# Twelve head pairs in one loop, with batch 0's first product in one piece

## The chip, the cores and the metric

The kernel runs on one core of a Trainium2 chip. The metric is the device time of one execution in microseconds (us).

Engine names in the profile: PE is TensorE (PEld its weight loads), DVE is VectorE, ACT is ScalarE, POOL is GpSimd, SP is SyncE, which here issues the DMAs of q, k, v, of the output and of the transposes. POOL issues the DMAs of the weights.

## The reference

Attention over 8 batches, 12 heads, 448 positions and a head size of 64, with one added to each softmax denominator; its output, laid out as 3584 rows of 768, goes through a two-layer network with the Mish function (2048 wide).

```python
scores = scale * np.matmul(q, k.transpose(0, 1, 3, 2))
m = np.max(scores, axis=-1, keepdims=True)
e = np.exp(scores - m)
attn = e / (np.sum(e, axis=-1, keepdims=True) + np.exp(-m) + 1e-09)
attn_out = np.matmul(attn, v)

x = attn_out.transpose(0, 2, 1, 3).reshape(B * S, H * D)
h = x @ w_in
sp = np.where(h > 20.0, h, np.log1p(np.exp(np.minimum(h, 20.0))))
g = h * np.tanh(sp)
return g @ w_out
```

## The kernel before

**Pairs and steps.** Work goes by head pairs: 48 of them, six to a batch. A pair has seven 128-row tiles of scores (its two heads have 896 rows) and is done in four steps: three with two tiles, the last with one. A step's scores lie in one of three PSUM tiles of two banks (`sc_tiles`), taken in turn, so scores can be three steps ahead of the exps (`scores_ahead`).

**The life of a pair.** `load_pair` loads q, k, v in f32 (three DMAs on SP's queue). `cast_pair` makes bf16 of them (three GpSimd instructions). `transpose_pair` turns q and k on PE, and `evac_qk` brings them from PSUM to SBUF, scaled; from pair 12 on (`DIAG_FROM`) q is laid out blockwise with zeros, so that one matmul makes a tile for both heads, and VectorE writes it (two memsets for each of the first three such pairs, two scalings). `scores` issues PE's matmuls and VectorE's reduction for the row maximum (L270). `exps` issues ScalarE's exponentials (L283) with the row sums; after the last step comes `expm`, the exponential of the negated maximum. `denominators` adds and inverts on VectorE. `normalise` multiplies the seven tiles of `en` by the reciprocals (L317 on VectorE, or L315 on GpSimd after a small copy of the reciprocals, L308). Then `en` is turned into `eT`, by one DMA transpose on SP's queue (L321) or by PE (`turn_on_pe`: seven transposes for each of four blocks j, each copied out of PSUM by VectorE, L336). `av_pair` multiplies `eT` with v (eight matmuls, L358); its result is copied to `xT` (L367).

**The two products.** `mm1_mish` makes one 128-wide block of the first product out of `xT` (six matmuls, L382) and applies Mish on ScalarE (L388); a batch has 16 blocks. Mish and the exponential need different activation tables, so ScalarE loads a table at each change between them. `mm2_part` gives pieces of the second product (L446), to be put between other work.

**PSUM.** Besides the three score tiles there are two one-bank tiles `mo`, which q/k transposes, turns, `av` and the products share. A result that is to be copied out is put on the list `late`; `flush_late` issues these copies, and `mo_take` does so when no `mo` is free.

**The order.** No scheduler decides: each engine carries out its instructions in the order in which the program issues them (`manual_schedule`).

- Pairs 0 to 5 (`HEAD = HP`) go through a loop of their own. In step 0 of pair p, pair p+4 is loaded, p+3 is cast and one piece of a weight is loaded; pair p-1 is normalised in step 1; `av` of pair p-3 is issued in step 3.
- Then come units of three pairs. A unit runs the twelve steps of its pairs with pieces of the second product as filler between them (`plan`), and then eight blocks of the first product, behind which the three pairs are normalised and the q and k of the next unit are turned. Unit 2 (pairs 6 to 8) and unit 3 (pairs 9 to 11) have no filler and do the two halves of batch 0's first product. From unit 4 (`first_mm2`) on the second product runs along, and in units from there GpSimd normalises the third pair.
- PE turns pairs 5, 6 and 7 (`BY_PE`) during units 2 and 3; all others are turned by DMA.
- In these early units the `xT` copies are VectorE's; in the head loop they are ScalarE's (`act=True`).

The weight `w_in` comes in twelve pieces (a quarter of the columns, two of the six row blocks each), `w_out` in eight.

Of the kernel before, what the change touches and what calls it, by code (L numbers as in the profile page):

```python
# [9 lines left out]
FP32 = mybir.dt.float32  # L10
# [5 lines left out]
UNIT_PAIRS = 3  # L16
# [3 lines left out]
def kernel(  # L20
# [73 lines left out]
    DIAG_FROM = 2 * HP  # L94
    q_diag = [
# [32 lines left out]
    def w_pieces():  # L128
        c_in, c_out = d_ff // 4, NH
        for i in range(4):  # L130
            for a in range(0, DM_T, 2):
                yield (
                    w_in_sb[:, a : a + 2, i * c_in : (i + 1) * c_in],
                    moe_w_in[a * 128 : (a + 2) * 128, i * c_in : (i + 1) * c_in],
                )
# [31 lines left out]
    def transpose_pair(p, bank=None):  # L167
# [3 lines left out]
        ps = mo_take() if bank is None else sc_tiles[2][:, bank, :]  # L171
        ps_k = sc_tiles[1][:, bank, :] if bank is not None else mo_take() if p == 0 else ps
# [56 lines left out]
    def scores(idx):  # L229

        p, s = divmod(idx, STEPS)
        if s == 0:
            if p < HP or p % UNIT_PAIRS == 0:
                for nm in ("negm", "sums", "expm", "den", "rden"):
                    stats[nm] = st_pool.tile([128, UNIT_PAIRS, NTILE], FP32, tag=nm, name=nm)
            at = 0 if p < HP else p % UNIT_PAIRS
# [6 lines left out]
        if s == STEPS - 1 and p in av_with:  # L243
            av_pair(av_with.pop(p), bank=sc[:, 1, :])
# [30 lines left out]
    def exps(idx):  # L275
# [13 lines left out]
        if s == STEPS - 1 and p < HP:  # L289
# [12 lines left out]
    def normalise(p, dma=True, on_pool=False):  # L302
# [6 lines left out]
        for i in range(NTILE):  # L309
# [6 lines left out]
            else:  # L316
                nc.vector.tensor_scalar(scalar2=None, op0=ALU.mult, **args)  # L317
        eT = eT_pool.tile([128, NT, 2 * S], BF16, tag="eT", name="eT")
        st["eT"] = eT
        if dma:  # L320
            nc.sync.dma_start_transpose(  # L321
                out=eT.rearrange("c j (i q) -> c (j i) q", q=128),
                in_=en.rearrange("q j i c -> q (j i c)"),
            )

# [49 lines left out]
    def mm1_mish(b, ff):  # L375
# [3 lines left out]
        spare = ff % FF_U == 2  # L379
# [113 lines left out]
    W_AT = ({5: 1, 9: 1}, {1: 1, 5: 1, 7: 1, 9: 1, 11: 1}, {1: 1, 3: 1, 5: 1, 7: 1})  # L493
# [9 lines left out]
    cast_pair(2)  # L503


    for p in range(HEAD):
        for s in range(STEPS):
            if s == 1 and p == 0:
                transpose_pair(p + 2)
            exps(p * STEPS + s)  # L510
            if p == 0 and s == 0:
                evac_qk(1, act=True)
            if s == 1:
                evac_qk(p + 2, act=True)
            if s:
                flush_late()
            scores_ahead(HEAD * STEPS + 3)
            if s == (2 if p == HEAD - 1 else 0):
                load_pair(p + 4)
            if s == 0:  # L520
                cast_pair(p + 3)
                load_w(1)
                if p:
                    denominators(att[p - 1])
            if s == 1:
                if p:
                    normalise(p - 1)
            if s == 3 and p + 3 < HEAD + 2:
                transpose_pair(p + 3)
            if s == 3 and p >= 3:  # L530
                av_pair(p - 3, act=True)
    denominators(att[HEAD - 1])
    normalise(HEAD - 1, dma=HEAD - 1 not in BY_PE)

    for u in range(UNITS_PER_B, N_UNITS + 2 * UNITS_PER_B):
# [10 lines left out]
        for n in range(steps):  # L546
            pi, s = divmod(n, STEPS)
            p, idx = p0 + pi, p0 * STEPS + n
            late_tp = u == UNITS_PER_B and n == STEPS
            if late_tp:  # L550
                transpose_pair(p0 + 2)
            exps(idx)
            if late_tp:
                evac_qk(p0 + 2)
# [87 lines left out]
```

## Time and profile before

| | |
|---|---|
| median of 3 runs | 493.48 us (492.4 to 493.5) |
| the profiled execution | 492.95 us, its span 491.2 us, mean granted clock 0.99 |
| busy, share of the span | PE 92%, DVE 72%, ACT 71%, POOL 31% |
| DMA | 92.19 MB; hardware queue 81.7%, software queue 9.1% of 16 engines' time |
| exps of pairs 0 to 5 | 8.05 to 45.2 us |
| unit 2: exps, then product | 45.2 to 65.1, to 77.5 us |
| unit 3: exps, then product | 77.5 to 98.5, to 110.5 us |
| unit 4: exps | 110.5 to 125.6 us |

All details of the profile come from one execution, so times within it are set against its own 492.95 us. In a row of instruction groups, "x7" is the number of instructions and the figure before the engine's name their time together. The digits of a slice are tenths of its time.

### The profile page before, as it was taken

What the parts mean: (1) busy time and instruction counts of PE and PEld (TensorE: products, weight loads), DVE (VectorE), ACT (ScalarE), POOL (GpSimd) and SP (SyncE); (2) the same over time, 40 slices, a digit from 0 to 9 for tenths busy, and PEclk for the clock granted to TensorE, in tenths of its full rate; (3) what the DMA queues carried; (4) which work ended last, traced back from release to release, by engine and by line L of the source; (5) the groups of instructions that cost most, each with busy time, mean ns of one, the idle gap of its engine ahead of it and who ended that gap; (6) DMA issues with size and microseconds to landing.
All of it is one profiled execution on the core that took longest, in us unless ns stands there. A gap on an engine that the chain in (4) does not pass through costs nothing.

```text
span 491.2 us, 8805 instructions
## 1 busy us (share of the span) xinstructions
PE 451.8 (92%) x2992; PEld 249.3 (51%) x2992; DVE 352.7 (72%) x714; ACT 349.5 (71%) x906; POOL 152.1 (31%) x252
## 2 busy tenths in 40 slices
PE   4466995898999999999999999999999999999996
PEld 2222442454555555555555555556555565556563
DVE  4898987788868787878788786878797878420021
ACT  5988675768788887979697978888797979502300
POOL 4622270701433534252523324253435230300000
PEclk9999998799999999999999999999999999999999
DMA  8999999999999999899999979898999796780112
GB/s 221 207 211 214 245 212 154 239 166 223 190 231 249 215 226 195 240 187 250 147 247 198 216 175 206 209 216 234 176 260 174 170 177 141 132 157 21 45 37 93
DMA packets 209452, 92.19 MB, mean 188 GB/s; under 512 B 166272, under 2 KB 205952, under 8 KB 209408
## 3 DMA queue, kind: packets, MB, share of 16 engines
q1 hardware_dynamic: 201920, 85.35, 81.7%
q0 software_dynamic: 7488, 6.29, 9.1%
q8 instruction: 23, 0.38, 0.3%
q14 instruction: 21, 0.17, 0.1%
HBM read 45.61 MB, written 11.01 MB: 115 GB/s over the span
## 4 chain that ended last, share of the span: by engine, by line
PE 74%; DVE 10%; ACT 7%; DMA 6%; issue 2%; SPq 1%; POOL 0%; DVEq 0%; ACTq 0%
PE mo L446 26%; PE mo L382 24%; PE sc L249 9%; ACT en L283 6%; PE sc L358 6%; DVE negm L270 5%; DMA eT<-en 5%; PE sc L382 3%; DVE en L317 3%; PE sc L179 3%; PE mo L358 1%; DMA k_f<-in_k_dram 1%; DVE xT L367 1%; SPq L121 1%; PE mo L332 0%
## 5 line engine op out<-in xcount | busy, mean ns | idle before, releaser
L283 ACT ACTIVATE en<-sc,negm 128x448 bf16<-128x448 f32 x336 | 209.6, 638 | 31.9 <-DVE negm L270 14.5
L270 DVE TENSOR_REDUCE negm<-sc 128x2 f32<-128x896 f32 x192 | 182.6, 969 | 56.3 <-PE sc L249 44.9
L446 PE MATMUL mo<-w_out_sb,gT 128*128 128x384 bf16 (+1 forms) x896 | 142.1, 303 | 0.0
L382 PE MATMUL mo<-xT,w_in_sb 128*128 128x448 bf16 x672 | 140.3, 352 | 0.4 <-DVE xT L367 0.4
L388 ACT ACTIVATE gT<-mo 128x448 bf16<-128x448 f32 x112 | 59.4, 543 | 72.4 <-PE mo L382 72.2
L446 PEld LDWEIGHTS <-gT 128*128 128x128 bf16 x896 | 84.0, 98 | 46.8 <-issue 1.3
L382 PEld LDWEIGHTS <-w_in_sb 128*128 128x128 bf16 x768 | 72.8, 98 | 64.6 <-issue 3.8
L315 POOL TENSOR_SCALAR en<-en,rden 128x448 bf16<-128x448 bf16 x84 | 52.8, 650 | 93.8 <-DVE rden L308 86.9
L162 POOL CAST q_bf<-q_f 112x512 bf16<-112x512 f32 x47 | 28.9, 616 | 160.2 <-DMA q_f<-in_q_dram 151.1
L249 PE MATMUL sc<-kT,qd 128*128 128x448 bf16 x252 | 71.6, 354 | 1.5 <-DVE qd L210 0.7
L317 DVE TENSOR_SCALAR en<-en,rden 128x448 bf16<-128x448 bf16 x252 | 69.7, 347 | 0.9
L283 ACT ACTIVATION_READ_ACCUMULATOR en<-sc,negm 128x1 f32 x336 | 69.4, 207 | 0.0
L433 DVE COPY o_sb<-mo 128x384 f32<-128x384 f32 (+1 forms) x64 | 32.1, 502 | 41.3 <-PE mo L446 41.2
L249 PEld LDWEIGHTS <-qd 128*128 128x128 bf16 x252 | 23.9, 97 | 31.8 <-issue 13.8
L358 PE MATMUL sc<-eT,v_bf 112*64 112x448 bf16 x288 | 34.1, 357 | 2.0 <-ACT en L283 1.8
L164 POOL CAST v_bf<-v_f 112x512 bf16<-112x512 f32 x48 | 29.6, 616 | 15.4 <-DMA v_f<-in_v_dram 14.1
L255 PE MATMUL sc<-kT,qd 64*128 64x448 bf16 x36 | 17.7, 508 | 17.9 <-ACT en L283 16.1
L358 PEld LDWEIGHTS <-v_bf 112*64 112x64 bf16 x384 | 21.0, 115 | 25.4 <-issue 18.7
L163 POOL CAST k_bf<-k_f 112x512 bf16<-112x512 f32 x47 | 29.0, 617 | 5.1 <-DMA k_f<-in_k_dram 4.0
L210 DVE TENSOR_SCALAR qd<-sc 64x448 bf16<-64x448 bf16 x72 | 27.8, 386 | 0.9
L218 ACT COPY kT<-sc 128x448 bf16<-128x448 bf16 x39 | 20.8, 534 | 7.0 <-PE sc L179 7.0
L446 PE MATMUL mo<-w_out_sb,mid 128*128 128x384 bf16 x128 | 24.9, 326 | 0.0
(50 smaller groups left out, 307.3 us busy)
## 6 DMA issues: line engine op xcount, KB each, us to landing
q_f<-in_q_dram SPq DMA_DIRECT2D x48, 224.0 KB, 5.1
k_f<-in_k_dram SPq DMA_DIRECT2D x48, 224.0 KB, 5.3
v_f<-in_v_dram SPq DMA_DIRECT2D x48, 224.0 KB, 5.5
w_in_sb<-in_moe_w_in_dram POOLq DMA_DIRECT2D x12, 256.0 KB, 5.8
w_out_sb<-in_moe_w_out_dram POOLq DMA_DIRECT2D x8, 384.0 KB, 7.5
out_dram<-o_sb SPq DMA_DIRECT2D x7, 336.0 KB, 3.4
out_dram<-o_sb SPq DMA_DIRECT2D x8, 288.0 KB, 4.5
out_dram<-o_sb SPq DMA_DIRECT2D x8, 240.0 KB, 3.4
```

The source lines that it names most:

```text
L163: cast_k(out=k_bf, in_=k_f.rearrange(by_t, t=NT))
L164: nc.gpsimd.tensor_copy(out=v_bf, in_=v_f)
L249: nc.tensor.matmul(sc[:, bk, 0:S], lhsT=qT[:, i].rearrange("d h r -> d (h r)"), rhs=kT, start=True, stop=True,)
L270: nc.vector.tensor_reduce(out=negm, in_=sc[:, 0 : len(cols), 0:S], axis=AX.X, op=ALU.max, negate=True)
L283: nc.scalar.activation(out=st["en"][:, :, c, 0:SP_], in_=sc[:, bk, 0:S].rearrange("q (j c) -> q j c", j=NT), func=AF.Exp, bias=st["negm"][ ...
L315: nc.gpsimd.tensor_scalar(scalar2=1.0, op0=ALU.mult, op1=ALU.mult, **args)
L317: nc.vector.tensor_scalar(scalar2=None, op0=ALU.mult, **args)
L358: nc.tensor.matmul(av[h * 64 : (h + 1) * 64, 0:S], lhsT=v_bf[:, h, j * D : (j + 1) * D], rhs=e_h, start=(j == 0), stop=(j == NT - 1),)
L382: nc.tensor.matmul(h_ps[:, 0:S], lhsT=w_in_sb[:, dm, ff * 128 : (ff + 1) * 128], rhs=xT[b][:, dm, :], start=(dm == 0), stop=(dm == DM_T - 1),)
L388: nc.scalar.activation(out=gT[b][:, ff, :], in_=h_ps[:, 0:S], func=AF.Mish)
L433: nc.vector.tensor_copy(out=o_sb[:, cols], in_=st["o"][:, 0:n_cols])
L446: nc.tensor.matmul(st["o"][:, 0:n_cols], lhsT=src[:, ff, c0 : c0 + 128], rhs=w_out_sb[:, ff, cols], start=(ff == 0), stop=(ff == FF_T - 1),)
```

## The change

- `HEAD` becomes 12: the pairs of batches 0 and 1 all go through a new `head_pair`. Units begin at unit 4.
- Behind pair 6 (`FIRST` is 7) stands `first_product`: all 16 blocks of batch 0's first product. Blocks 0 and 1 start with five of six row blocks in a score tile's banks while pair 5's `av` is still to come. Pair 6 is normalised by VectorE there, pairs 7 and 8 have q and k turned there, and the first three scores of pair 7 are issued between the last blocks.
- In `head_pair`, GpSimd normalises the last three of seven tiles (`ON_POOL`), VectorE the first four: two in step 0, two in step 1. This concerns pairs 0 to 5 and 7 to 10; pairs 6 and 11 are normalised by VectorE alone.
- PE turns pairs 4, 5, 7 and 8, two blocks in step 2 and two in step 3 of the next pair; the other head pairs are turned by DMA.
- `av` of a pair that was turned by DMA is issued in step 2 of the third pair after it, of pair 4 in step 0 of pair 6; `av` of pairs 6 to 8 goes with the last scores of pairs 9 to 11, into a free bank. All but pair 5's `xT` copies among these are ScalarE's, and so are q's and k's evacuations of pairs 2 to 11.
- q and k of pairs 12 to 14 are turned in the steps of pairs 10 and 11 and of unit 4 instead of behind the first product.
- No pairs are loaded in the steps of pairs 3 to 6; `first_product` issues the loads of pairs 7 to 10 at once.
- Pieces of `w_in` are half of the columns by one row block; loads of both weights are spread anew (`W_AT`).
- The first piece of the second product (rows 0 to 127, half the columns, 16 matmuls) goes between the steps of pairs 10 and 11. Units 4 and 5 have two whole halves and three whole halves left, instead of two and a half and three and a half, and the two quarter pieces of 192 columns become one half piece.

The core of the diff; not shown are the new `w_pieces`, `HEAD` in place of `HP` in `scores` and `exps`, the choice of banks in `transpose_pair`, and `turn`, which is the second half of `normalise`:

```diff
+    def normalise_tiles(p, tiles, on_pool=False):
+        st = att[p]
+        en = st["en"]
+        if on_pool:
+            st["rden2"] = st_pool.tile([128, NTILE], FP32, tag="rden2", name="rden2")
+            nc.vector.tensor_copy(out=st["rden2"], in_=st["rden"])
+        for i in tiles:
+            args = dict(
+                out=en[:, :, i, 0:SP_], in0=en[:, :, i, 0:SP_],
+                scalar1=st["rden2" if on_pool else "rden"][:, i : i + 1],
+            )
+            if on_pool:
+                nc.gpsimd.tensor_scalar(scalar2=1.0, op0=ALU.mult, op1=ALU.mult, **args)
+            else:
+                nc.vector.tensor_scalar(scalar2=None, op0=ALU.mult, **args)
...
+    def mm1_first(b, banks, last):
...
+        for ff in range(len(banks)):
+            part(ff, range(DM_T - 1))
+        last()
+        flush_late()
+        for ff in range(len(banks)):
+            part(ff, (DM_T - 1,))
+            nc.scalar.activation(out=gT[b][:, ff, :], in_=banks[ff][:, 0:S], func=AF.Mish)
...
-            plan[u0] = [(0, i, 0, 2) for i in range(2)] + [(0, 2, 0, 1)]
-            plan[u0 + 1] = [(0, 2, 1, 1)] + [(0, i, 2, 2) for i in range(3)]
+            plan[u0] = [(0, i, 0, 2) for i in (1, 2)]
+            plan[u0 + 1] = [(0, i, 2, 2) for i in range(3)]
...
-    HEAD = HP
-    BY_PE = {HEAD - 1: 1, HEAD: 0, HEAD + 1: STEPS}
-    AV_AT = {0: {5: 3, 7: 4, 10: 5}, 1: {3: 8, 6: 6, 10: 7}}
+    FIRST = HP + 1
+    BY_PE = (4, 5, 7, 8)
+    ON_POOL = 3
...
+    def head_pair(p):
+        for s in range(STEPS):
+            exps(p * STEPS + s)
+            if s == 0 and p == 0:
+                evac_qk(1, act=True)
+            if s == 2 and p + 2 != FIRST and p + 2 != FIRST + 1:
+                evac_qk(p + 2, act=True)
+            flush_late()
+            if p >= HEAD - 2:
+                early.popleft()()
+            scores_ahead((FIRST if p < FIRST else HEAD + 1) * STEPS)
+            load_w(W_AT.get((p, s), 0))
+            if s == 0:
+                if p + 4 < FIRST or p >= FIRST:
+                    load_pair(p + 4)
+                if p + 3 < FIRST or p >= FIRST:
+                    cast_pair(p + 3)
+                if p < FIRST and p - 2 in BY_PE:
+                    av_pair(p - 2, act=True)
+                if p and p != FIRST:
+                    denominators(att[p - 1])
+                    normalise_tiles(p - 1, range(NTILE - ON_POOL, NTILE), on_pool=True)
+                    normalise_tiles(p - 1, range(0, 2))
+            if s == 1:
+                if p and p != FIRST:
+                    normalise_tiles(p - 1, range(2, NTILE - ON_POOL))
+                    turn(p - 1, dma=p - 1 not in BY_PE)
+                if p + 2 != FIRST and p + 2 != FIRST + 1:
+                    transpose_pair(p + 2)
+            if s == 2 and 3 <= p < FIRST and p - 3 not in BY_PE:
+                av_pair(p - 3, act=True)
+            if s >= 2 and p - 1 in BY_PE:
+                for j in (2 * s - 4, 2 * s - 3):
+                    turn_on_pe(p - 1, j)
+
+    def first_product(p):
+
+        for i in range(4):
+            load_pair(p + 1 + i)
+        denominators(att[p])
+        mm1_first(
+            0, [sc_tiles[1][:, i, :] for i in range(2)],
+            lambda: (flush_late(), av_pair(p - 1, bank=sc_tiles[2][:, 0, :])),
+        )
+        normalise(p)
+        for ff in range(2, FF_T):
+            mm1_mish(0, ff, banks=False)
...
+            if ff in (3, 5, 7):
+                cast_pair(p + 1 + (ff - 3) // 2)
+            if ff in (8, 10):
+                q = p + 1 + (ff - 8) // 2
+                transpose_pair(q, bank=(ff - 8) // 2, banks=(0, 2))
+                evac_qk(q, act=True)
+            if ff >= FF_T - 5 and ff % 2:
+                scores_ahead((p + 1) * STEPS + (ff - FF_T + 7) // 2)
...
+    av_with.update({p: p - UNIT_PAIRS for p in range(FIRST + 2, HEAD)})
+    early = deque()
     for p in range(HEAD):
...
+        head_pair(p)
+        if p == FIRST - 1:
+            first_product(p)
+            early.extend(fn for fn, _ in mm2_part(0, 0, 0, 2))
     denominators(att[HEAD - 1])
-    normalise(HEAD - 1, dma=HEAD - 1 not in BY_PE)
-
-    for u in range(UNITS_PER_B, N_UNITS + 2 * UNITS_PER_B):
+    normalise(HEAD - 1)
+    gather_mid(0)
+    assert not early
+
+    for u in range(first_mm2, N_UNITS + 2 * UNITS_PER_B):
...
+            if u == first_mm2 and n == 2:
+                evac_qk(p0 + 2, act=True)
...
+            if u == first_mm2 and n == 1:
+                transpose_pair(p0 + 2)
```

More of the change, by code (lines that the diff above doesn't have):

```diff
@@ L94 @@
     DIAG_FROM = 2 * HP
+    HEAD = 2 * HP
     q_diag = [
@@ L372, in av_pair, with part, mm1_mish @@
         del att[p], casted[p], qkT[p]
-    def mm1_mish(b, ff):
+    def mm1_first(b, banks, last):
+        gT[b] = gT_pool.tile([128, FF_T, S], BF16, tag="gT", name="gT")
+        def part(ff, dms):
+            for dm in dms:
+                nc.tensor.matmul(
+                    banks[ff][:, 0:S],
+                    lhsT=w_in_sb[:, dm, ff * 128 : (ff + 1) * 128],
+                    rhs=xT[b][:, dm, :],
+                    start=(dm == 0), stop=(dm == DM_T - 1),
+                )
[6 more added lines that the diff above has]
+            nc.scalar.activation(out=gT[b][:, ff, :], in_=banks[ff][:, 0:S], func=AF.Mish)
+    def mm1_mish(b, ff, banks=True):
         if ff == 0:
@@ L378, in mm1_mish @@
         flush_late()
-        spare = ff % FF_U == 2
+        spare = banks and ff % FF_U == 2
         h_ps = sc_tiles[0][:, 0, :] if spare else mo_take()
```

97 lines of the change are left out of this document (32 added, 65 removed), and 3 rows, old and new, of the table W_AT.

## The prediction

> **What bounds the kernel now.** The slices of the page come first: which engine carries which part.
>
> ```profile
> PE   4466995898999999999999999999999999999996
> DVE  4898987788868787878788786878797878420021
> ACT  5988675768788887979697978888797979502300
> PEclk9999998799999999999999999999999999999999
> ```
>
> From slice 10 (about 124 us) PE is at 9 to the end; before it VectorE and ScalarE lead and PE has holes. The change lies in the holes. The busy times by stage split them:
>
> ```profile
> 49.90:65.10 15.20, 14.30 (x85) 7.34 (x84) 13.97 (x25) 10.97 (x35) 5.02 (x9) 1.00 1.10 257
> 65.10:77.50 12.40, 10.87 (x85) 5.97 (x83) 10.30 (x25) 8.09 (x13) 6.35 (x11) 1.00 1.09 160
> 77.50:98.50 21.00, 13.95 (x95) 7.90 (x95) 15.47 (x26) 13.36 (x43) 9.56 (x15) 0.76 1.23 209
> 98.50:110.50 12.00, 11.38 (x79) 6.25 (x78) 10.83 (x31) 8.15 (x14) 0.00 (x0) 1.00 1.08 166
> 110.50:125.60 15.10, 13.04 (x88) 7.24 (x87) 12.91 (x24) 13.65 (x44) 4.50 (x8) 1.00 1.02 231
> 138.00:166.00 28.00, 28.00 (x190) 15.45 (x189) 21.69 (x43) 23.37 (x61) 11.22 (x19) 1.00 1.05 235
> ```
>
> After the window come its length and the busy time of PE, PEld, DVE, ACT, POOL. The rows are pairs 6 to 8; half of batch 0's first product; pairs 9 to 11; the other half; pairs 12 to 14; the steady state (PE 28.00 of 28.00). In both product stages VectorE is busy too (10.3 of 12.4, 10.8 of 12.0): normalising of three pairs and the next q stand behind matmuls. Pairs 9 to 11 are the poor stage, 21.0 us against 15.2. ScalarE's waits say why:
>
> ```profile
> ACT en L283 <- DVE negm L270: 9.4, 12, 2.4
> ACT en L283 <- PE mo L332: 7.6, 2, 5.1
> ACT gT L388 <- PE mo L382: 5.7, 9, 1.0
> ```
>
> The 7.6 are two waits (5.1 and 2.5) in that stage, behind turns on PE; in the longer one PE itself stands until 85.0 in front of an `eT` that is still in a DMA. What the change can win is there; what it can lose is the work that VectorE now does beside the product.
>
> As mark I take the moment when pair 11's `xT` is copied (L367, 124.13 + 0.6 = 124.7). From there PE is fed without a hole, so a shift of the mark is a shift of the end, but for the lighter fifth unit below.
>
> **Pairs 0 to 4.** ScalarE per pair: seven exps at 0.615 from one to the next, 0.1 for expm, two evacuations at 0.42: 5.25 us. VectorE: three reductions at 1.05 and one at 0.57, 0.4 for the denominators, 0.16 for the copy `rden2` (row L308), four tiles at 0.26 instead of seven: 5.3. GpSimd: three tiles at 0.65, three casts at 0.62: 3.8 of 6, and the weight pieces (0.72 each) have room; they need 5.8 us to land and are due at the product, 15 us on. SP has four transposes there and loads 7 to 10 behind them, needed 20 us later. All this is hidden. New is a wait on ScalarE: `av_pair` is issued in step 2 and its `xT` copy stands ahead of pair p+1's exps. After step 2's exps PE does the scores (0.5) and eight matmuls (1.7, row L358 at half clock): 2.75 us with hand-overs, while ScalarE has 0.85 + 0.7 to do. Pairs 3 and 4 pay 0.8 to 1.2 each. Sum: pair 4 ends at 38.5 (before 38.7).
>
> **Pairs 5 and 6.** Pair 5 has no q to evacuate, but pair 2's `xT` copy comes before its last exp: 3.7 + 2.75 + 0.4 + 0.7 = 7.5 us, less 0.25 where the copy is met early. In pair 6 the copies of pairs 4 and 3 stand between the exps. Pair 4's needs all four turns of pair 4, and each pair of turns (0.95 each) needs its two banks copied by VectorE (0.61 each) first: 2.5 us of idle ScalarE, in all 2.5 + 2.5 + 0.4 + 1.25 + 0.4 + 0.7 = 7.7. Pair 6 ends at 53.5; before, pair 6 ended at 52.9.
>
> **The product.** On PE stand now the four turns of pair 5 with their copies (2.7), ten matmuls (1.9), pair 5's `av` (0.95), its `xT` on VectorE (0.6) and the last slice (0.4). The first turns start about 1.1 before pair 6's last exp ends, so 5.4 us of these 6.5 pass until the third block begins. Then 14 blocks at 1.17 (six matmuls, rows of 98.5 to 110.5) = 16.4, two q/k transposes and three scores at 0.45 = 2.25, the last Mish 0.6, one table load 1.28. Pair 7 begins at 79.5. Before, the two product stages cost 12.4 + 12.0 with two table pairs; here 26.0 with one. The saved table load (2.56) goes to the chain ahead of the blocks.
>
> **Pairs 7 to 14.** In the product VectorE has four copies of turned tiles, one `xT`, pair 6's seven tiles and three reductions (2.4 + 0.6 + 1.8 + 3.1 = 8 of 26 us); all else follows it. From 79.5 to the mark: 21 reductions at 1.05 and 8 at 0.57 = 26.6; eight copies of turned tiles at 0.61 = 4.9; 23 tiles at 0.26 = 6.0; denominators and copies 2.6; q of pairs 12 to 14 (two memsets, two scalings, 1.4 a pair) 4.2; three `xT`, the gather, two `o_sb` 3.3. Together 47.6. ScalarE has 41 and is no bound. At the 92% that the densest stretch of before shows (13.97 of 15.20) this takes 51.7.
>
> Do three tiles on GpSimd take 0.78 off VectorE? These two stretches speak of it:
>
> ```profile
> 18.72 2.31 DVE L317 TENSOR_SCALAR en<-en,rden 128x448 bf16<-128x448 bf16 x7
> 25.13 1.80 DVE L317 TENSOR_SCALAR en<-en,rden 128x448 bf16<-128x448 bf16 x7
> ```
>
> The first has one GpSimd cast (0.62) inside it, the second none: 0.5 more. Nothing in the trace has GpSimd tiles beside VectorE tiles; by the cast it costs 0 to 0.5 for each tile, 0 to 2.0 a pair. I take one wait a pair, since two of the four tiles stand right beside GpSimd's 1.95 us and two behind a reduction: 0.5 for pairs 7 to 10, 2.0. (The Trainium skill, "SBUF — State Buffer", "Who interferes with whom", has VectorE and GpSimd share a port pair as an exclusive lock, the second fully blocked; the 0.5 agrees, and by that rule the offloading is nearly given back.)
>
> The mark: 79.5 + 51.7 + 2.0 = 133.2, against 124.7: +8.5. Unit 5 loses one quarter part (16 matmuls of 192 columns at 0.1 to 0.11 = 1.6 to 1.8); PE is full there, ScalarE nearly (I take 1.5). Unit 4's smaller filler lies beside VectorE's list: nothing. Net +7.0: the profiled execution of 492.95 goes to 500.0. It lies 0.5 under the median of the three runs, so 500.5.
>
> **Bounds.** Low: turns and `av` at full clock (0.55 and 0.95) bring pair 7 to 77.7; the list at its smallest pitches is 46.4, and 1.3 of pair 7 can't be filled, since its first three reductions are done: 125.4, +0.7, less 1.8: 492.4. High: the product starts at half clock (+2), 4 us of waits for turns, every tile blocked (+6), unit 5 wins nothing: 79.5 + 2 + 51.7 + 2 + 4 + 6 = 145.2, +20.5, with nothing from unit 5: 514. All at once is unlikely; half of the excess over 500.5 gives 507 and a little.
>
> **Rivals.**
>
> *Faster: ScalarE sets the pace of pairs 7 to 11.* If VectorE's list fits into gaps, pairs take 5.7 (5.25 and an `xT` copy): 79.5 + 28.5 = 108.0 for the start of pair 12, and 14.2 (13.65 busy, no table load ahead) to the mark: 122.2, -2.5, less 1.5: 489.5. For it: the wait of 5.1 has no DMA to wait for any more. Against: 47.6 us of list in 42.7 us. It decides only if the list is under 43. 0.13.
>
> *No change:* the low bound above, 492 to 495. VectorE would have to work at 98%. 0.11.
>
> *PE's clock.* In 82 to 92 us, where turns stood, the granted clock was 0.50 and seven transposes took 0.99 instead of 0.55. Pairs 8 and 9 hold eight turns, two `av` and eight scores: at half clock they cost 8 x 0.44 + 2 x 0.75 (1.7 against 0.95) + 8 x 0.19 (0.55 against 0.36) = 6.5 more, of which I let VectorE's list hide a good third: +4, 504.5. For it: pair 7 leaves PE half idle. Against: the clock came back at 92 amid turns and scores. 0.13. (The Trainium skill, "TensorE: Matmul & The Clock Gate", "Part 4: PE-mode transpose", says that transposes don't count as busy for the gate; by that the turns would stay slow, and the time is this rival's.)
>
> *The offloading does nothing:* every tile of pairs 7 to 10 is blocked, +6, 506.5. For it the 2.31, and a longest tile of 0.93 against a median of 0.33; against, GpSimd's tiles span only part of VectorE's. 0.10.
>
> The forecast, VectorE bound behind the product, has 0.53, with 495 to 504 as its own range; 0.3% is about what a measurement of this kernel can tell from no change. Faster 0.13 and a little for what I overlooked: 0.14; same 0.11; slower 0.75. The range, from 491.5 to 508, leaves out most of the faster rival and the rest of the worst case.
>
> **What would show it.** Right: pair 7's first exp near 79.5; VectorE over 90% busy from pair 8 to pair 14 and largely idle in the product; ScalarE idle before `xT` L392 and waiting for reductions; the mark near 133; PE full from there. Wrong: pairs 7 to 11 at under 6 us each (the faster rival); turns of 0.99 throughout (the clock); VectorE's tiles near 0.8 (the offloading). A first product that begins by 56 or ends by 75 would refute the chain that I put ahead of it.

## The result and the profile after

The changed kernel takes 524.38 us (median of 4 runs, 520.7 to 525.9), the kernel before 493.49 (median of four, one run more than in the table above): a ratio of 1.061, interval 1.053 to 1.068. The prediction said 500.5 and a range of 491.5 to 508. The direction is right, the size is not. The profiled execution is the slowest of the four (525.92) and has a span of 524.1 against 491.2: 32.9 us to be accounted for.

The slices of the page after, to be laid beside those of before (a slice is now 13.1 us):

```profile
PE   4552289675779899999999999999999999999996
DVE  4884072488778787878887878787878787730121
ACT  5983145776567979797969787888788888703200
PEclk9999989869889999999999999999999999999999
```

The fourth and fifth digit (39 to 65 us) are new: PE at 2, VectorE at 4 and 0, ScalarE at 3 and 1. No engine does much there. A second poor stretch begins with the eighth digit (92 us): PE at 5 to 7 until 157 us, and a lower clock. The stages in numbers (window, its length, busy time of PE, PEld, DVE, ACT, POOL, then the granted clock, the busy share of the DMA engines, GB/s; the share adds up the times of packets that overlap, so it can be above 1):

```profile
38.50:61.70 23.20, 3.89 (x16) 1.42 (x16) 7.08 (x14) 4.37 (x15) 7.33 (x13) 1.00 1.19 123
...
78.70:99.00 20.30, 18.13 (x107) 9.23 (x107) 6.02 (x9) 11.65 (x21) 4.90 (x8) 1.00 1.11 223
99.00:111.00 12.00, 7.08 (x41) 3.79 (x41) 7.92 (x15) 11.32 (x37) 2.77 (x4) 0.53 0.12 29
111.00:139.00 28.00, 17.76 (x137) 9.65 (x136) 22.29 (x50) 16.37 (x53) 16.22 (x25) 0.90 0.80 133
139.00:157.80 18.80, 14.85 (x86) 6.97 (x86) 15.19 (x30) 13.08 (x42) 4.29 (x7) 0.91 0.90 201
170.30:185.60 15.30, 13.98 (x87) 7.28 (x86) 11.05 (x16) 13.81 (x44) 4.85 (x10) 1.00 1.00 249
```

In the first row all five engines stand most of the time while the DMA engines are fully busy (1.19). ScalarE's waits name the place:

```profile
ACT xT L392 <- PE mo L383: 22.2, 4, 17.9
ACT kT L223 <- DVE qd L215: 8.9, 3, 4.5
...
ACT xT L392 <- DVE negm L275: 7.2, 3, 2.8
```

The 17.9 is one wait: the copy of pair 2's `xT`, ahead of pair 5's last exp. The chain of waits shows what ends it (start, length, what):

```profile
38.56 23.12 DMA eT<-en
61.68 0.04 issue
61.72 1.70 PE mo L383 x8
```

Pair 2's transpose was issued at 38.56 and landed at 61.68. In the kernel before, the first five transposes land 7.4 to 9.9 us after their issue.

With the prediction's own marks, the 32.9 are made up so:

| | forecast | measured |
|---|---|---|
| pair 4 ends | 38.5 | 38.4 |
| pair 5 | 7.3 | 26.1 |
| pair 6 | 7.7 | 6.6 |
| pair 6's end to pair 7's first exp | 26.0 | 28.0 |
| pair 7's first exp | 79.5 | 99.1 |
| from there to the mark | 53.7 | 58.8 |
| the mark (before: 124.7) | 133.2 | 157.85 |
| behind the mark, against before | -1.5 | -0.1 |

So 19.6 of the excess over the forecast arise ahead of pair 7, nearly all in pair 5; 5.1 in pairs 7 to 14; 1.4 in unit 5.

### The profile page after: what moved, and what is told of

It is laid out like the page before. It is cut to its first block, busy times and chain, and to the rows that moved or that the text cites. A ratio compares the mean times of both kernels' runs of the same rounds, so it can differ in the third digit from the quotient of the medians.

```text
span 524.1 us, 8847 instructions
## 1 busy us (share of the span) xinstructions
PE 455.7 (87%) x3004; PEld 251.6 (48%) x3004; DVE 347.7 (66%) x695; ACT 351.0 (67%) x918; POOL 170.9 (33%) x282
## 3 DMA queue, kind: packets, MB, share of 16 engines
q0 software_dynamic: 5952, 6.29, 8.4%
HBM read 45.61 MB, written 11.01 MB: 108 GB/s over the span
## 4 chain that ended last, share of the span: by engine, by line
PE 72%; DVE 8%; ACT 6%; DMA 4%; issue 2%; POOL 0%; DVEq 0%; ACTq 0%; POOLq 0%
PE mo L428 24%; PE mo L492 24%; PE sc L254 8%; PE sc L383 7%; ACT en L288 5%; DMA eT<-en 4%; DVE negm L275 3%; PE sc L428 3%; PE sc L184 3%; PE mo L357 1%; PE mo L383 1%; DVE xT L392 1%; DVE en L322 1%; PE sc L406 1%; DVE qd L215 1%
## 5 line engine op out<-in xcount | busy, mean ns | idle before, releaser
L492 PE MATMUL mo<-w_out_sb,gT 128*128 128x384 bf16 (+1 forms) x880 | 144.4, 307 | 3.8 <-ACT kT L223 2.8
L434 ACT ACTIVATE gT<-mo 128x448 bf16<-128x448 f32 x112 | 59.5, 543 | 75.0 <-PE mo L428 74.6
L492 PEld LDWEIGHTS <-gT 128*128 128x128 bf16 x880 | 82.5, 98 | 51.8 <-issue 6.9
L320 POOL TENSOR_SCALAR en<-en,rden 128x448 bf16<-128x448 bf16 x84 | 52.6, 647 | 105.0 <-DVE rden L313 105.0
L479 DVE COPY o_sb<-mo 128x384 f32<-128x384 f32 (+1 forms) x63 | 32.0, 508 | 42.7 <-PE mo L492 42.5
L322 DVE TENSOR_SCALAR en<-en,rden 128x448 bf16<-128x448 bf16 x182 | 49.1, 343 | 0.9
L383 PE MATMUL sc<-eT,v_bf 112*64 112x448 bf16 x320 | 39.2, 366 | 2.7 <-ACT en L288 2.5
L347 POOL TENSOR_SCALAR en<-en,rden 128x448 bf16<-128x448 bf16 x30 | 21.1, 713 | 49.5 <-DVE rden L340 26.2
L260 PE MATMUL sc<-kT,qd 64*128 64x448 bf16 x36 | 17.4, 495 | 17.9 <-ACT en L288 17.4
L215 DVE TENSOR_SCALAR qd<-sc 64x448 bf16<-64x448 bf16 x66 | 25.5, 386 | 0.8
L383 PE MATMUL mo<-eT,v_bf 112*64 112x448 bf16 x64 | 9.7, 438 | 18.4 <-DMA eT<-en 17.8
```

The lines of the kernel that those rows point to most:

```text
L215: nc.vector.tensor_scalar(out=qd[rows, :, h, :], in0=q_ps[rows, 0:S].rearrange("d (i r) -> d i r", i=QB), scalar1=SCALE, scalar2=None, op0 ...
L320: nc.gpsimd.tensor_scalar(scalar2=1.0, op0=ALU.mult, op1=ALU.mult, **args)
L383: nc.tensor.matmul(av[h * 64 : (h + 1) * 64, 0:S], lhsT=v_bf[:, h, j * D : (j + 1) * D], rhs=e_h, start=(j == 0), stop=(j == NT - 1),)
L434: nc.scalar.activation(out=gT[b][:, ff, :], in_=h_ps[:, 0:S], func=AF.Mish)
L479: nc.vector.tensor_copy(out=o_sb[:, cols], in_=st["o"][:, 0:n_cols])
L492: nc.tensor.matmul(st["o"][:, 0:n_cols], lhsT=src[:, ff, c0 : c0 + 128], rhs=w_out_sb[:, ff, cols], start=(ff == 0), stop=(ff == FF_T - 1),)
```

## Experiments

T0 to T3 are the DMA transposes of pairs 0 to 3; a landing is counted from the issue. **Theory W**: weight pieces that are underway at the same time make the transposes slow. **Rival S**: T2 is merely issued late, because GpSimd's tiles stand behind casts that wait for load 6 (SP's queue, behind T0). Where an expectation speaks of pair 4's start at 42.5, it is that of pair 5: I had counted the pairs one too low there.

**e1_pieces**: other packets, same bytes, same places.

```diff
-        c_in, c_out = d_ff // 2, NH
-        for i in range(2):
-            for a in range(DM_T):
+        c_in, c_out = d_ff // 4, NH
+        for i in range(4):
+            for a in range(0, DM_T, 2):
...
```

> The changed kernel with the w_in pieces of the kernel before (a quarter of the columns, two row blocks: packets of 1024 bytes instead of 2048), issued at the same places. In the changed kernel pair 2's transpose is issued at 38.6 us and lands 23.1 us later, at 61.7, and ScalarE stands 17.9 us before the xT copy that needs it. Theory W (the large packets of the weight pieces, issued at 38.5, 41.5 and 47.4 beside it, hold the transpose up): its landing takes 10 to 14 us, so ScalarE's stall falls by 9 or more and the time from 524.4 to about 515. Rival S (it is late because it is issued late, behind GpSimd's casts and load 6): landing time unchanged within 3 us, time 521 to 526.

Measured: 520.31 us. T2 lands after 15.9 instead of 23.1, but T3 after 19.0 instead of 15.6; from T2's issue to T3's landing it is 26.0 us and was 26.3. So the size of the packets (2048 or 1024 bytes) is not it. T2's landing came nearer to the 10 to 14 that the expectation asked for, but T3 paid for it.

**e2_load6**: load 6 in pair 1's step 0, ahead of T0.

```diff
-                if p + 4 < FIRST or p >= FIRST:
+                if p + 4 < FIRST - 1 or p >= FIRST:
                     load_pair(p + 4)
+                if p + 5 == FIRST - 1:
+                    load_pair(FIRST - 1)
```

> The changed kernel with pair 6 loaded beside pair 5, in pair 1's step 0, so ahead of the first transpose on SP's queue instead of behind it. The casts of pair 6 on GpSimd then need not wait for data at 27 to 34 us, and pair 2's three GpSimd tiles end near 32 instead of 38.5. Rival S (late issue): pair 2's transpose is issued near 32 and lands within 8 us, most of the 17.9 us stall is gone: 507 to 512. Theory W (weight packets): it is issued 6.5 us earlier, but the pieces at 38 to 47 still meet pair 3's transpose and perhaps its end: 515 to 518. A third, that SP itself was the bound (its transposes hold it for 5.4 us each): issue at 38 or later as now, no gain.

Measured: 521.77 us. T2 is issued at 35.4, 3.2 us earlier, and little is won: GpSimd is earlier too, its pieces now meet T1 (22.0) and T2 (20.7). Rival S gets no support: an earlier issue among the pieces moves the stall to another transpose. (T2 was to be issued near 32; it was held until T1 had let go of SP at 35.3.)

```profile
ACT xT L392 <- PE mo L383: 18.0, 5, 11.2
```

**e3_wlate**: three pieces in pairs 2 and 3, the rest from pair 5's step 2 on.

```diff
-        (2, 0): 1, (2, 2): 1, (3, 0): 1, (3, 2): 1, (4, 0): 1, (4, 2): 1,
-        (5, 0): 1, (5, 2): 1, (6, 0): 1, (6, 2): 1,
+        (2, 0): 1, (2, 2): 1, (3, 0): 1, (5, 2): 2, (6, 0): 3, (6, 2): 2,
```

> The changed kernel with three weight pieces in pairs 2 and 3 and the other seven moved to pairs 5 and 6, so that none is issued at 38 to 50 us beside the transposes of pairs 2 and 3. Theory W: pair 2's transpose, still issued at 38.6, lands in 6 to 9 us, at 45 to 48; the stall of 17.9 falls to about 3, and the time to 509 to 511, unless the product then waits for its weights (its first block needs six pieces; the last comes 8 us after pair 6's step 2). Rival S: the stall falls by under 4 us: 520 or more.

Measured: 509.73 us, as theory W had it; ratio to the kernel before 1.032, interval 1.023 to 1.042: 14.7 of the 31 us are gone by moving weight loads. T2 is issued even later (39.3) than in the changed kernel and yet lands in time, which refutes rival S. What the trace has on the transposes issued at 38 to 44 us, first of the changed kernel (there 38 to 50), then of e3; the last row is the time from issue to landing:

```profile
L330 SPq DMA_TRANSPOSE eT<-en x2: 10463/12042/13622, 38.6 to 49.2; - x2
...
DMA to landing us min/median/max: 15.6/19.4/23.1
```

```profile
L330 SPq DMA_TRANSPOSE eT<-en x2: 4177/4222/4267, 39.3 to 43.7; - x2
...
DMA to landing us min/median/max: 6.1/6.1/6.2
```

The first numbers are the time (ns) for which SP itself is held by the issue: 10.5 and 13.6 us against 4.2. So a transpose that has company also delays whatever is queued behind it on SP. ScalarE's longest wait before an `xT` copy falls from 17.9 to 3.8, and that one belongs to T1, which still had two pieces and load 6 beside it and took 12.8.

**e4_nopool**: all seven tiles by VectorE.

```diff
-    ON_POOL = 3
+    ON_POOL = 0
...
-                    normalise_tiles(p - 1, range(NTILE - ON_POOL, NTILE), on_pool=True)
+                    pass
```

> The changed kernel with all seven tiles of every head pair normalised by VectorE, as in the kernel before; GpSimd keeps the casts and the weight pieces. Rival S: pair 2's transpose no longer waits for GpSimd's casts and tiles, is issued near 32 and lands before the weight pieces; the stall of 17.9 loses 10 or more, less the 0.8 us a pair that VectorE gains in work in pairs 7 to 10 (3 us, less any blocking by GpSimd that goes): 511 to 515. Theory W: issued earlier by 6 and still slow beside the pieces: 517 to 520. If the port were what cost, VectorE's four tiles a pair would shorten from their 0.5 us by as much as they are blocked, and pairs 7 to 11 would not lengthen.

Measured: 519.88 us. Freed of its tiles, GpSimd issues eight pieces in one go at 33 to 37 us, T2 (issued at 34.0) takes 17.7, T3 without pieces 6.1. From pair 7 to the mark it takes 64.1 instead of 58.8, in one execution each; kernels that do the same work in this stretch as the changed one took up to 62.5 (below), so the offloading is worth 1.6 to 5 there.

**e7_wlast**: no piece before step 2 of pair 4, then all ten.

```diff
-        (2, 0): 1, (2, 2): 1, (3, 0): 1, (3, 2): 1, (4, 0): 1, (4, 2): 1,
-        (5, 0): 1, (5, 2): 1, (6, 0): 1, (6, 2): 1,
+        (4, 2): 6, (5, 2): 4,
```

> The changed kernel with all ten weight pieces of the first pairs issued in step 2 of pairs 4 and 5, none before. In e3_wlate pair 1's transpose, beside three pieces, still landed 12.8 us after its issue, at 40.3, ScalarE stood 3.8 for it, and pair 6 ended at 56.2. Theory W: it lands 6 to 8 us after its issue, pair 4 starts at 38.5 to 39.5 instead of 42.5, and pair 6 ends at 53 to 54.5, as the prediction had it for a head loop in which the transposes are hidden; pair 7 starts near 80; time 506 to 508. Rival (the loads of pair 6 beside it hold it): it takes 10 us or more as in e3, time as e3, 509 to 511. If the pieces come too late for the product, PE waits for w_in at its first block.

Measured: 523.47 us, for the opposite of the hoped reason, and the clearest case of all. The first fence is the transposes T0 to T2, the second T3, which meets all ten pieces:

```profile
L330 SPq DMA_TRANSPOSE eT<-en x3: 4313/4648/4860, 20.7 to 33.0; - x3
...
DMA to landing us min/median/max: 6.1/6.2/8.0
```

```profile
L330 SPq DMA_TRANSPOSE eT<-en x1: 12718/12718/12718, 38.8 to 38.8; - x1
...
DMA to landing us min/median/max: 26.4/26.4/26.4
```

Pair 5 starts at 39.7, as the expectation had it; then T3's product with v waits and ScalarE with it (14.3 in one wait). The pieces suffer too: the first two land after 4 and 8 us, the other eight after 18 to 21.

**e10_split**: four pieces in pairs 0 and 1, six from pair 5's step 1 on.

```diff
-        (2, 0): 1, (2, 2): 1, (3, 0): 1, (3, 2): 1, (4, 0): 1, (4, 2): 1,
-        (5, 0): 1, (5, 2): 1, (6, 0): 1, (6, 2): 1,
+        (0, 2): 1, (1, 0): 1, (1, 2): 2, (5, 1): 2, (6, 0): 3, (6, 2): 1,
```

> The changed kernel with four weight pieces issued in pairs 0 and 1, before the first transpose, and six from pair 5's step 1 on, behind the last of the four DMA transposes; e3_wlate with none at 25 to 35 us. Theory W: the four transposes of pairs 0 to 3 land 6 to 8 us after their issue, pair 4 starts at 39 to 40 instead of 42.5, pair 6 ends at 53 to 54, pair 7 starts near 80; time 506 to 508 against e3's 509.7. Rival (the early pieces delay the loads of pairs 3 to 5 and thus the casts, or the first product waits for its fifth piece): as e3 or more, 509 to 512.

Measured: 509.77 us, as e3: a miss by 2 to 4. T2 and T3 land after 6.1. But two of the four early pieces slipped on GpSimd's queue to 20.5 and 21.1, beside T0 (10.9), which held SP, so T1 was issued 3 us later, and pair 5 starts at 41.6 instead of 42.5.

**e13_qload**: e3, where no weight piece runs at 38 to 48 us, with the loads of pairs 7 and 8 put there, on GpSimd's queue.

```diff
+            if (p, s) in ((3, 2), (4, 2)):
+                load_pair(p + 4, nc.gpsimd)
...
```

> The kernel e3_wlate (509.73 us; transposes of pairs 2 and 3 land 6.2 and 6.1 us after their issue) with the loads of pairs 7 and 8 (1.34 MB in f32, packets of 1024 bytes) issued by GpSimd in step 2 of pairs 3 and 4, at 38 to 45 us, where the changed kernel has its weight pieces. Theory W in its wide form (any bytes beside a transpose hold it up alike): the two transposes take 12 us or more, time 514 to 522. Its narrow form (only weight pieces do, in 2048-byte packets that took 172 ns each): 7 to 10 us, as beside loads in the kernel before, time 509 to 511.

```profile
L330 SPq DMA_TRANSPOSE eT<-en x2: 5255/9992/14729, 38.1 to 43.5; - x2
...
DMA to landing us min/median/max: 12.0/16.3/20.6
```

Measured: 523.39 us. T2 takes 12.0 beside plain f32 loads (the first weight piece was issued 1.7 us before it landed); T3's 20.6 has weight pieces beside it as well. On GpSimd's queue these loads went in packets of 4096 bytes, not of 1024 as the expectation says; with e1 that makes three sizes, and none of them free. It is the wide form: transfers beside a transpose, and not the weights as such. A single piece and some loads of SP's own queue cost less: so it was in the kernel before, with 7.4 to 9.9. Whether the queue matters, or only the amount, isn't shown: SP's queue never had as much beside a transpose.

**The stretch from pair 7 to the mark.** Ten more kernels look for the 5.1 that are missing there. The table gives the median time and the length of that stretch in the one profiled execution. The changed kernel, e1, e2, e3, e7 and e10 have the same work in this stretch and took 58.8 to 62.5, and the runs of e11 lie between 505.1 and 508.2: a difference of under 4 us in the stretch, or of under 3 in the time where ranges overlap, shows nothing by itself. The changed kernel's 58.8 is the shortest of those six.

| kernel | us | stretch |
|---|---|---|
| changed kernel | 524.38 | 58.8 |
| e3_wlate | 509.73 | 59.3 |
| e10_split | 509.77 | 60.3 |
| e5: e3, k copied first | 507.30 | 58.1 |
| e6: e3, pairs 7, 8 turned by DMA | 513.38 | 63.9 |
| e8: e3, xT copies on VectorE | 513.54 | 64.1 |
| e9: e3, xT copies one step later | 514.24 | 61.1 |
| e11: e10, e9 and e5 together | 506.85 | 56.2 |
| e12: e11, scores issued twice | 507.86 | 58.2 |
| e14: e11, pairs 7, 8 turned by DMA | 508.56 | 59.5 |
| e15: e14, scores issued twice | 509.33 | 57.4 |
| e16: e11, five tiles on GpSimd | 506.96 | 57.4 |
| e17: e11, no tile on GpSimd | 507.53 | 57.0 |

**e5_ktfirst**, in `evac_qk`, for pairs 12 to 14:

```diff
             qkT[p] = (qd, kT)
+            if act:
+                nc.scalar.copy(kT, k_ps[:, 0:S])
...
-        else:
+        elif p < DIAG_FROM or not act:
             nc.scalar.copy(kT, k_ps[:, 0:S])
```

> The kernel e3_wlate (509.73 us) with one more edit: for pairs 12 to 14, ScalarE's copy of k is issued ahead of VectorE's scalings of q from the same PSUM bank instead of behind them. In e3 ScalarE waits 8.9 us in three such copies for VectorE, ahead of the next exps; pair 7's first exp is at 82.6, the mark (pair 11's xT copied) at 141.9, 59.3 us apart where the prediction had 53.7, and VectorE is busy 49 of them. Theory L (ScalarE's stand there breaks the ring of exps, scores and reductions): 59.3 falls to 53 to 56, time 503 to 507. Rival (VectorE's list alone sets these pairs, and the wait only moves to the next reduction): 58 to 60, time 508.5 to 511.

The 8.9 us before `kT` are gone from the waits. In their place stands this row (it was 7.3, 23 times, in e3); the line numbers are two higher:

```profile
ACT en L290 <- DVE negm L277: 11.5, 29, 2.4
```

The stretch hardly moves, so in this execution the wait mostly changed its name. That the time gained 2.4 isn't shown: the two runs of e5 are 505.2 and 509.4, those of e3 509.2 and 510.3.

**e6_dma78**:

```diff
-    BY_PE = (4, 5, 7, 8)
+    BY_PE = (4, 5)
```

> The kernel e3_wlate with pairs 7 and 8 turned by DMA instead of PE; pairs 4 and 5 stay on PE. VectorE loses eight copies of turned tiles (4.7 us), PE 56 transposes, SP gets two transposes. If VectorE's list sets pairs 7 to 14, the stretch from pair 7 to the mark falls from 59.3 by 4 to 5, time 505 to 506. If PE's clock at the turns does (0.57 and 0.72 in 82 to 102 us of e3), the clock rises and the gain is 5 or more. If ScalarE's waits for other engines' order do (k copies, xT copies), 0 to 2: 508 to 510. The transposes meet weight pieces and may take 10 us or more; they have 25 us before their product with v.

It took 4.9 us of copies off VectorE, and the time is 3.7 longer (513.2 and 513.5 against 509.2 and 510.3), outside every range that was expected. The transposes of pairs 7 and 8 met pieces of w_out and landed after 12.9 us each: theory W once more. The clock lay at 0.50 to 0.61 in 92 to 112.

**e8_xtdve** (first line) and **e9_xtlater** (the rest; `held` is a list like `late`):

```diff
-            av_pair(av_with.pop(p), act=p < HEAD, bank=sc[:, 1, :])
+            av_pair(av_with.pop(p), act=False, bank=sc[:, 1, :])
...
-        late.append(evac)
+        (held if act and bank is not None else late).append(evac)
...
+            if s == 2 and held:
+                held.popleft()()
             flush_late()
```

> The kernel e3_wlate with the xT copies of pairs 6 to 8 done by VectorE instead of ScalarE. In e3 ScalarE waits 7.6 us in front of these three (put down to VectorE's reduction of the same score tile) and then copies 1.3. VectorE gets 1.8 more. If ScalarE's stand there is what lengthens pairs 9 to 11 (9 to 10 us each against 5.7 of pairs 7 and 8): 3 to 6 less, 504 to 507. If VectorE's list does, 1 to 2 more: 511 to 512.

> The kernel e3_wlate (509.73 us) in which ScalarE copies the xT of pairs 6 to 8 behind the exps of step 2 instead of ahead of them. In e3 and in the kernels after it ScalarE finishes step 1's exps and then stands 3 to 4 us before that copy, while step 2's scores are long reduced: PE has two turns, the product with v and step 3's scores to do first, VectorE the reduction of step 3. Theory X (this stand, three times in pairs 9 to 11, is what lengthens them to 9 to 10 us): the stretch from pair 7 to the mark falls from 59.3 to 50 to 54, time 501 to 505. Rival (VectorE's list or PE at half clock sets these pairs anyway; taking the k copies' wait away in e5 moved only 1 us): 57 or more, 507 to 510.

Both are misses of mine, slower than e3 in every run. In e9 the xT copy no longer stands there, and the k copies' wait grows from 8.9 to 15.5.

**e11_all**: e10's places for the weights, e9's and e5's edits.

> e10_split, e9_xtlater and e5_ktfirst together: no weight piece beside a transpose, ScalarE's xT copies behind step 2's exps, k copied ahead of q's scalings. If the three causes are separate, their gains over e3 add: 3 (early transposes), 5 to 8 (xT copies), 1 to 2 (k copies): 497 to 501, near the prediction's 500.5 and still over the kernel before. If VectorE's list sets pairs 8 to 14 once ScalarE no longer stands there, VectorE is over 92% busy in them and the sum is 2 to 4 less: 501 to 505.

506.85 us, ratio 1.027, interval 1.023 to 1.031: the lowest median of all these, still slower than the kernel before, and a miss, since both sums of the expectation were lower. Against e10, which has the weights at the same places, it is 2.9 faster, and the ranges don't overlap: taking both of ScalarE's waits away gives that much. Its 56.2 comes from the fastest of its four runs (505.07) and flatters it.

**e12_twice** (below, around the two score matmuls of steps 0 to 2); **e14_alldma** is e6's edit in e11, **e15_dmatwice** both.

```diff
+            for _ in range(2 if FIRST <= p else 1):
                 nc.tensor.matmul(
...
```

> The kernel e11_all (506.85 us, 56.2 from pair 7 to the mark, granted clock 0.53, 0.79, 1.00, 0.83, 0.83 in 82 to 132 us by tens) with every score matmul of pairs 7 to 11 issued twice, steps 0 to 2; the second overwrites the first with the same numbers. Theory C (PE at a low clock sets these pairs, and it is low because PE stands): the clock comes to 0.9 or more and the stretch falls by 1 to 4, time 503 to 506. Rival V (VectorE and ScalarE set them): the clock may rise, the stretch stays or lengthens by up to 2 (30 matmuls of 0.19 to 0.36): 507 to 509.

> The kernel e11_all with pairs 7 and 8 turned by DMA instead of PE (VectorE loses eight copies, 4.9 us). Theory V (VectorE's list sets the stretch, 90% busy in 92 to 132 us): 56.2 falls by 3 to 5, time 502 to 504. Theory C (PE's clock): PE stands more, the clock stays at 0.5 to 0.7, the stretch lengthens as it did from e3 to e6 (by 4.6): 508 to 512.

> The kernel e14_alldma with the score matmuls of pairs 7 to 11 issued twice as in e12. Theory C: the clock is held up, and what e14 lost comes back; 2 to 5 us faster than e14, at best 500 to 503. Theory V: as e14, up to 2 slower. If e14 is slow because its transposes land late beside w_out pieces, neither helps, and PE or ScalarE wait for eT in it.

e12 did not do what it was for. Here are 102 to 112 us of e11, then of e12: PE is busier, the clock (the third number from the end) is lower.

```profile
102.00:112.00 10.00, 7.55 (x62) 3.52 (x60) 8.41 (x19) 5.25 (x17) 6.78 (x11) 1.00 0.60 84
```

```profile
102.00:112.00 10.00, 9.00 (x59) 3.70 (x56) 7.19 (x17) 4.75 (x16) 5.56 (x10) 0.66 0.58 81
```

From 82 to 132 us the clock is 0.74 instead of 0.80. So it says nothing on what a higher clock would bring. e15 is as e14. In e14 the transposes of pairs 7 and 8 land after 11.7 and 11.4, and PE stands for them (98 to 114 us):

```profile
PE sc L385 <- DMA eT<-en: 5.9, 2, 3.4
```

**e16_pool5** and, with 0 for 5, **e17_pool0**, in e11:

```diff
+                    n_pool = 5 if p > FIRST else ON_POOL
+                    if n_pool:
+                        normalise_tiles(p - 1, range(NTILE - n_pool, NTILE), on_pool=True)
...
+                    normalise_tiles(p - 1, range(2, NTILE - n_pool))
```

> The kernel e11_all with five instead of three tiles of pairs 7 to 10 normalised by GpSimd. VectorE loses eight tiles, 2.6 us by the row of 0.33 each; GpSimd gets eight of 0.65. Theory V (VectorE's list sets the stretch of 56.2): 53 to 54.5, time 504 to 505.5. If the tiles were blocked one for one by GpSimd's, nothing is won: 506 to 508. If GpSimd becomes late (casts of the next pair behind five tiles), turns wait for it: 508 or more.

> The kernel e11_all with all seven tiles of pairs 7 to 10 normalised by VectorE. VectorE gets twelve tiles, 3.1 to 4.0 us at 0.26 to 0.33, and loses four small copies of the reciprocals, 0.7. Theory V: the stretch goes from 56.2 to 58.5 to 60, time 509 to 511. If GpSimd's tiles block VectorE's one for one, it stays within 1: 506 to 508, and VectorE's tiles fall to 0.26 each from a mean of 0.41.

Eight tiles fewer and twelve more on VectorE: 57.4 and 57.0, both within 1.3 of e11, and times within 0.7 of it. As far as runs with this scatter can tell, VectorE's list does not set this stretch in e11.

## Why the prediction was wrong

**The step that failed** is in the paragraph on pairs 0 to 4: the weight pieces "have room; they need 5.8 us to land", SP's transposes stand there, "All this is hidden". I priced each queue by itself, GpSimd's pieces by GpSimd's time and the transposes by SP's order, and not what they do to each other on the DMA engines. Shown by e3, e7 and e13: a transpose without company lands after 6.1 us, and in these three runs, beside two or more transfers of GpSimd's queue, after 12.0 to 26.4. In the changed kernel that made pair 5 26.1 us long instead of 7.3. Where T2 and T3 have no company (e3, e10, e11), pair 5 takes 7.15 from its first exp to its last, and 9.3 to 11.6 from pair 4's end, since T0 or T1 still had some; pair 7 then begins at 81.1 in e11, where 79.5 was forecast and 99.1 measured.

The size can be worked out in part. Here are the DMA engines in e3 while T2 and T3 are underway with nothing beside them:

```profile
39.30:49.70 10.40, 6.65 (x35) 3.04 (x35) 5.30 (x12) 5.33 (x17) 5.62 (x9) 1.00 1.03 193
```

The transposes alone keep them busy (1.03), at 193 GB/s, so what others move comes on top. The six pieces beside T2 and T3 of the changed kernel count with the 1.57 MB that they write in bf16, but they read 3.15 MB in f32 (the page's HBM reads, 45.61 MB, are 33.03 for q, k and v and 12.58 for weights that count with 6.29). By what is read, the 123 GB/s of 38.5 to 61.7 us are 191: no less than for the transposes alone. An estimate from this: 3.15 MB at 191 GB/s take 16.5 us, and from T2's issue to T3's landing it is 26.3 us instead of 10.4, 15.9 more. e13 agrees (1.38 MB of loads at the 215 GB/s of 38.1 to 50.1 us are 6.4, and T2 took 5.9 longer). In e7 and e4 a piece cost less: ten cost T3 20.3, eight cost T2 11.6. So a piece beside a transpose cost it about 1.5 to 2.6 us.

The Trainium skill, "DMA: Bandwidth & Descriptors", "Queues, rings and completion order", has each DMA engine go round its queues packet by packet. The trace agrees in so far as transfers of GpSimd's queue and a transpose of SP's share the time of the engines (T2 beside f32 loads of GpSimd's queue: 12.0 instead of 6.1); that they alternate by packets no run here shows.

The kernel before had the warning: its transpose issued at 69.55 landed 15.4 later, with pieces issued at 64.5 to 71.0.

```profile
L321 SPq DMA_TRANSPOSE eT<-en x1: 12187/12187/12187, 69.5 to 69.5; - x1
...
DMA to landing us min/median/max: 15.4/15.4/15.4
```

The prediction even quotes the wait that this caused (5.1) as what the change could win, and doesn't ask why that DMA was slow. The upper bound of 514 had terms for the clock, turns and blocked tiles, but none for a DMA.

**Pairs 0 to 4, pair 6**: right (38.4 for 38.5; 6.6 for 7.7). The wait that the prediction found, `xT` copies ahead of the next exps, is the door by which the slow DMA reaches ScalarE: the changed kernel takes `av` of pair 2 in pair 5's step 2 and ScalarE stands for it, with the exps behind.

**The product**: 28.0 for 26.0, and 26.4 in e3 and in e11. Right. VectorE has 6.02 of 20.30 us to do there, so the idea that it lies idle beside the matmuls holds.

**Pairs 7 to 14**: 58.8 for 53.7. VectorE's list was about right (45.4 in this stretch, 47.6 forecast), its density was not: 92% assumed, 77% measured, 7.92 of 12.00 in 99 to 111 and 22.29 of 28.00 behind it. Pairs 7 and 8 go at ScalarE's pace (5.7 each, as the faster rival had it) and leave VectorE little to do; pairs 9 to 12 then take 8.3 to 10.6 each, and no engine is full. The chain of waits from 99 to 158 us goes in 192 pieces back and forth between engines: reductions 18.3%, exps 14.1%, the product with v 9.8%, turns 6.8%, and smaller ones. e16 and e17 speak against VectorE's list as the bound, for e11. PE's clock alone doesn't explain it either. These are pair 8 and pair 10 of the changed kernel (the clock is the third number from the end):

```profile
104.80:110.50 5.70, 4.10 (x22) 2.14 (x21) 4.61 (x11) 5.37 (x19) 2.27 (x4) 0.50 0.00 0
118.80:129.40 10.60, 5.88 (x54) 3.13 (x54) 8.87 (x20) 5.58 (x20) 7.42 (x12) 1.00 0.60 90
```

At half the clock a pair takes 5.7 us, at the full clock 10.6. That leaves the hand-overs between engines in this order; which of them it is stays open.

**The lock**: 2.0 us forecast for pairs 7 to 10, and VectorE did not pay them; but the lock is there, and in these pairs GpSimd paid. VectorE's four tiles a pair in pairs 0 to 5, the same in pairs 7 to 10, and GpSimd's three beside the latter (ns: least, median, most):

```profile
L349 DVE TENSOR_SCALAR en<-en,rden x24: 321/331/867, 18.1 to 70.0; 128x448 bf16<-128x448 bf16 x24
...
L349 DVE TENSOR_SCALAR en<-en,rden x16: 326/330/333, 108.0 to 135.9; 128x448 bf16<-128x448 bf16 x16
L347 POOL TENSOR_SCALAR en<-en,rden x12: 627/729/888, 108.2 to 135.8; 128x448 bf16<-128x448 bf16 x12
```

Of the 222 such tiles of VectorE in the changed kernel's trace, 14 last over 0.40 us (0.45 to 0.87), and beside each GpSimd has a cast, a tile or the issue of a weight piece underway; the tile mostly ends 0.13 after the GpSimd instruction that it waited for. In e4 one tile took 1.94 us, behind an issue and three casts. (In the prediction's stretch of 2.31 us, 0.4 are due to the cast and 0.1 to the issue of a piece that follows it.) In pairs 7 to 10 it is GpSimd's tiles, 0.63 alone, that stretch to 0.73 and 0.89. So one of the two waits, and small shifts decide which: the fourth tile starts some 0.15 us after one of GpSimd's in pair 0 and in pair 7 alike, and waits only in pair 0 (0.71). In e11 some of VectorE's tiles of pairs 7 to 10 wait as well (up to 0.72).

**Unit 5**: 1.5 forecast, 0.1 won. The row 170.3 to 185.6 above is its exps; the same stretch of the kernel before is this one:

```profile
137.20:152.50 15.30, 15.30 (x97) 7.93 (x95) 11.37 (x18) 14.06 (x45) 4.26 (x8) 1.00 1.06 244
```

PE lost 1.3 us of work and the stretch kept its 15.30: ScalarE, 13.8 to 14.1 of it busy, is then the likely bound; no run tests that. The prediction had noted "ScalarE nearly" and given the whole gain all the same.

**The rivals**: the faster one and no change fall. The clock was as low as that rival said (0.53 in 99 to 111), but pairs 7 and 8 took 5.7 us all the same; what it cost in the turns that run over into pair 9 (8.3 us, clock 0.82) can't be told from these runs. That the offloading does nothing because each of VectorE's tiles is blocked falls: none of the 16 was. It is worth 1.6 to 5 us in the changed kernel's order (e4) and nothing that can be seen in e11 (e17: 0.7 slower without it). With the transposes freed and ScalarE's two waits gone, e11's profiled execution lies 12.1 over that of before, and 7.0 were forecast: 1.6 of the rest lie ahead of pair 7, 2.5 behind it, 1.0 in unit 5.

## What to carry to other kernels

Price a DMA by what is underway beside it, not by its queue: list, for each transfer that work waits for, the others between its issue and its landing, and look in the trace of before for the one that was already slow. When loads are spread anew, check what they land beside, above all transposes that a copy ahead of other work waits for. An edit that lightens one engine gains only where no other engine fills the stretch nearly as much: compare the busy time of the second engine with the length of the stretch first.

## What was not expected of the hardware

- A DMA transpose of one pair lands after 6.1 us alone, and holds SP for 4.2; beside six weight pieces (each 256 KB in bf16, read as f32) it takes 15.6 to 23.1 and holds SP for 10.5 to 13.6, beside ten pieces 26.4 and 12.7. The other side pays as well (in e7 18 to 21 us for eight of the ten pieces; in the kernel before a piece mostly takes 4 to 7). The size of the packets made no difference that could be seen (e1).
- The transposes alone keep the DMA engines fully busy: a share of 1.03 at 193 GB/s in e3. The low rate beside the pieces (1.19 at 123) is mostly a matter of counting, since a casting load counts with what it writes.
- VectorE's bf16 tiles of 0.33 us and GpSimd's instructions block each other: one of the two is longer by what is left of the other (VectorE's up to 0.87, in e4 1.94; GpSimd's 0.73 and 0.89 instead of 0.63).
